# Output stage of a spectral layer: norms two tiles sooner, one norm on GpSimd, turns spread over tiles, one more tile's x added on TensorE

## The chip, the cores and the metric

One core of one Trainium2 chip runs the whole program. The metric is the device time of one execution in microseconds (us), lower is better. This document also measures *stage lengths* inside the profiles: from the first 128x256 matmul of an output stage to the first matmul of the MLP behind it. They repeat far better than the totals (the three kernels below that should have the same stage show 25.08 or 25.09 us six times), and the views of PE's waits name no transfer in that stretch. Each stage length comes from one profiled execution. "Fast" and "slow" are states of an execution: the one slow execution met here took 1254.71 us at a granted TensorE clock of 0.556, the fast ones of the same kernel 737.71 to 741.87 us at 0.992 to 0.995 (lib_switch).

Engines: TensorE (PE, with its weight loads PEld), VectorE (DVE), ScalarE (ACT), GpSimd (POOL), SyncE (SP).

## The reference, cut to what matters

```python
def reference(A_x, A_w_r, A_w_i, B_x, B_w1, B_b1, B_w2, B_b2):
    # _A_ref: rfft2 over (2048, 576), times a complex filter, irfft2
    # _B_ref: layernorm, x @ w1 + b1, gelu, @ w2 + b2     (576 -> 4608 -> 576)
    x = A_x
    x = x + _A_ref(_layernorm(x, axis=-1), A_w_r, A_w_i)
    x = x + _B_ref(_layernorm(x, axis=-1), B_w1, B_b1, B_w2, B_b2)
    x = x + _A_ref(_layernorm(x, axis=-1), A_w_r, A_w_i)
    x = x + _B_ref(_layernorm(x, axis=-1), B_w1, B_b1, B_w2, B_b2)
    return x
```

The Fourier transforms are matmuls with constant matrices. The **output stage** is the end of the inverse transform: for each of 16 tiles of 128 rows it makes the last two products, adds x, and, while that goes on, prepares the first four tiles (the "quad") for the MLP: layernorm, then a transposition ("turn") on PE. It runs twice, once per layer.

## The kernel before: the parts that matter

The program order is fixed by hand on every engine. PSUM is shared by a pool of three two-bank buffers (`big_ps`) and one of two small buffers (`sm_ps`). Cuts are marked.

```python
    class SpectralOut:
        early = (1, 2, 6, 10)          # tiles whose x is added by PE, not by VectorE

        def idft_v(self, n):           # first product of tile n: four 128x256 matmuls, cast by ACT
            pu = sm_ps([P, 2, 2, 128], F32) if fresh else self.st.pop(("pu", n))
            ...
            marks["u2", n] = nc.scalar.copy(out=u2[:], in_=pu[:]).ins

        def idft_v_rest(self, q):      # last 34 rows of four tiles: one buffer
            pr = sm_ps([P, 4, P], F32)
            ...                        # 64x128 matmuls
            nc.scalar.copy(out=u2r[:], in_=pr[:])

        def put_x(self, n):            # x of an early tile, four 128x288 matmuls
            po = big_ps([P, 2, 512])
            ...

        def idft_k(self, n):           # second product of tile n: six 128x288 matmuls
            ...

        def add(self, n):              # early: one ACT copy, two VectorE adds; else three adds
            ...

        def run_all(self, prep, loads):
            ...                        # sums for the moments: ACT, tiles 1 to 7
            pieces[10].append(prep.root)
            for i, m in enumerate((13, 14, 14)):
                pieces[m].append(lambda i=i: prep.turn(i, "act"))
            behind_add = {9: [prep.moments], 11: [prep.scale_sums, lambda: prep.norm(0, nc.vector)],
                          12: [lambda: prep.norm(2, nc.vector)]}
            pieces[12].append(lambda: prep.norm_act(1))
            pieces[13].append(lambda: prep.norm_act(3))
            ...
            for n in range(NT):
                if n == NT - 1:
                    prep.turn(3, "act")
                if n in self.early[2:]:
                    self.put_x(n)
                self.idft_k(n)
                self.add(n)
                for call in behind_add.get(n, ()):
                    call()
                if 0 < n < NT - 2:
                    self.idft_v(n + 2)
                if n % 4 == 1 and n + 3 < NT:
                    self.idft_v_rest(n // 4 + 1)
                for call in pieces[n]:
                    call()
            self.add(NT)

    class Prep:
        def norm_act(self, i):         # norm on ACT; the last 64 columns are copied on GpSimd
            ...
            nc.gpsimd.tensor_copy(out=xn[:, D:640], in_=xn[:, D - 64 : D])

        def norm(self, i, engine=nc.gpsimd):   # norm on VectorE, column copy on `engine`
            ...

        def turn(self, i, evac):       # five transpositions on PE, one copy out of PSUM
            pt = sm_ps([P, 5, P])
            for ci in range(5):
                nc.tensor.transpose(pt[:, ci, :], xn[:, ci * 128 : (ci + 1) * 128], ident[:])
            if evac == "act":
                nc.scalar.copy(out=self.yT[:, :, i * 128 : (i + 1) * 128], in_=pt[:])
```

A turn needs the *copied* last 64 columns of its tile for its fifth transposition. The MLP's first matmul needs all four turned tiles.

## Time and profile before

| | before |
|---|---|
| time, median of the 6 runs beside the changed kernel | 731.12 us (730.81 to 731.41) |
| span of the profiled run | 729.2 us |
| PE busy | 98% of the span |
| first output stage | 58.99 to 84.88: 25.89 us |
| second output stage | 414.52 to 440.41: 25.89 us |

The page of the kernel before, parts 1 and 4. Part 1 has each engine's busy time, its share of the span, and its number of instructions; part 4 says by engine what the chain of work that ended last was made of (a q behind an engine's name is its sequencer).

```profile
PE 718.1 (98%) x5078; PEld 456.9 (63%) x5078; DVE 267.0 (37%) x917; ACT 309.5 (42%) x534; POOL 79.5 (11%) x139
...
PE 95%; ACT 2%; DVE 1%; DMA 1%; issue 0%; SPq 0%; POOL 0%; ACTq 0%; POOLq 0%
```

PE bounds the kernel, so a change that takes no work off PE can only win what PE still waits for. Those places are seen in the timeline. Below is PE at the end of the first output stage, kernel before: start, length, engine, source line, operation, output and inputs, shape, count, and in brackets the idle time before it with what ended it. Line 895 is a turn, 753 the second product of a tile, 919 the MLP. (Lengths of PE overlap, so starts are what counts: the first row is 0.44 us long, and the next starts 0.28 us after it.)

```profile
82.06 0.44 PE L895 MATMUL pss_1479<-ident,xn 128*128 128x128 bf16 x5
82.34 0.44 PE L895 MATMUL pss_1486<-ident,xn 128*128 128x128 bf16 x5
83.66 0.44 PE L895 MATMUL pss_1493<-ident,xn 128*128 128x128 bf16 x5 [0.88 <-ACT yT_1408 L897]
...
84.88 0.38 PE L919 MATMUL psb_1514<-yT_1408,w_sb 128*128 128x512 bf16 x1
```

Two turns at once fill both small buffers; the third waits 0.88 us until ACT has copied one out. ACT is late because the last norm stands in front of its copies; this is ACT at that time:

```profile
82.14 0.88 ACT L862 ACTIVATE xn<-x_sb,shift,rs 128x576 bf16<-128x576 bf16 x1
82.91 0.69 ACT L897 COPY yT_1408<-pss_1479 128x640 bf16<-128x640 bf16 x1
83.48 0.72 ACT L897 COPY yT_1408<-pss_1486 128x640 bf16<-128x640 bf16 x1
84.13 0.69 ACT L897 COPY yT_1408<-pss_1493 128x640 bf16<-128x640 bf16 x1
```

### The profile page before, as it was taken

The numbers are of one execution on the slowest core, as the hardware profiler recorded it, in microseconds if no ns is written. First come the engines' busy times: TensorE is split into PE (matmuls) and PEld (weight loads), VectorE is DVE, ScalarE is ACT, GpSimd is POOL, SyncE is SP. The second block draws the span as 40 slices with busy tenths as digits, with TensorE's granted clock in tenths as the row PEclk, the third lists the DMA queues.
The fourth block names the chain that finished last, engine by engine and source line by source line (L and its number), as shares of the span: only waits on it lengthen the run. The fifth ranks groups of instructions, "written<-read, shape, count | busy, mean of one in ns | idle before, by whom it ended". The sixth has DMA issues, their size and how long they took to land.

```text
span 729.2 us, 12472 instructions
## 1 busy us (share of the span) xinstructions
PE 718.1 (98%) x5078; PEld 456.9 (63%) x5078; DVE 267.0 (37%) x917; ACT 309.5 (42%) x534; POOL 79.5 (11%) x139
## 2 busy tenths in 40 slices
PE   8999999999999999999999999999999999999998
PEld 5777645864587448744877674477447744774476
DVE  7894910664055504520367586011400140110011
ACT  7796764026411651156216686610550056005600
POOL 4240112002000200000006301200100010000000
PEclk9999999999999999999999999999999999999999
DMA  9788345211111111100217402530102010200000
GB/s 291 215 194 202 141 150 194 66 44 54 37 39 50 55 32 41 47 7 1 59 40 235 134 2 71 188 115 18 44 1 45 17 45 1 45 19 8 1 17 17
DMA packets 52722, 54.33 MB, mean 75 GB/s; under 512 B 31576, under 2 KB 43624, under 8 KB 52664
## 3 DMA queue, kind: packets, MB, share of 16 engines
q1 hardware_dynamic: 43784, 25.99, 13.5%
q0 software_dynamic: 8448, 26.96, 11.7%
q8 instruction: 40, 0.66, 0.4%
q10 hardware_dynamic: 432, 0.58, 0.2%
q14 instruction: 18, 0.15, 0.1%
HBM read 29.31 MB, written 8.59 MB: 52 GB/s over the span
## 4 chain that ended last, share of the span: by engine, by line
PE 95%; ACT 2%; DVE 1%; DMA 1%; issue 0%; SPq 0%; POOL 0%; ACTq 0%; POOLq 0%
PE psb_4486 L966 1%; PE psb_6902 L966 1%; PE psb_6304 L966 1%; PE psb_5706 L966 1%; PE psb_4228 L966 1%; PE psb_4100 L966 1%; PE psb_3294 L966 1%; PE psb_2492 L966 1%; PE psb_2126 L966 1%; PE psb_1998 L966 1%; PE psb_7654 L966 1%; PE psb_7577 L966 1%; PE psb_7500 L966 1%; PE psb_7185 L966 1%; PE psb_7108 L966 1%; PE psb_6587 L966 1%
## 5 line engine op out<-in xcount | busy, mean ns | idle before, releaser
L966 PEld LDWEIGHTS <-h_sb 128*128 128x128 bf16 x2304 | 224.9, 98 | 57.8 <-issue 0.2
L919 PEld LDWEIGHTS <-w_sb 128*128 128x128 bf16 x1152 | 109.5, 98 | 142.4 <-issue 17.2
L875 DVE TENSOR_SCALAR xn<-x_sb,mv,rs 128x576 bf16<-128x576 bf16 x24 | 9.4, 427 | 67.2 <-DMA quad_1818<-xn 28.9
L333 DVE BATCH_NORM_STATS2 stats<-x_sb 128x6 f32<-128x288 bf16 x78 | 30.8, 437 | 0.0
L927 PEld LDWEIGHTS <-w1r_sb 64*128 64x128 bf16 x288 | 10.8, 94 | 24.5 <-issue 17.0
L961 DVE TENSOR_TENSOR xb<-x_sb,b_bc 128x576 f32<-128x576 bf16 x32 | 24.0, 749 | 0.0
L878 POOL COPY xn<-xn 128x64 bf16<-128x64 bf16 x24 | 6.4, 268 | 150.7 <-DVE xn L875 150.7
L654 PEld LDWEIGHTS <-h_sb 128*128 128x128 bf16 x160 | 15.4, 97 | 5.5 <-DVE shared_721 L639 0.6
L933 ACT ACTIVATE h_sb<-psb_6064,b_sb 128x512 bf16<-128x512 f32 x2 | 1.3, 684 | 37.9 <-PE psb_6064 L927 37.9
L933 ACT ACTIVATE h_sb<-psb_7260,b_sb 128x512 bf16<-128x512 f32 x2 | 1.3, 684 | 37.8 <-PE psb_7260 L927 37.8
L933 ACT ACTIVATE h_sb<-psb_6662,b_sb 128x512 bf16<-128x512 f32 x2 | 1.3, 684 | 37.8 <-PE psb_6662 L927 37.8
L989 DVE TENSOR_TENSOR x_sb<-psb_7500,xb 128x576 bf16<-128x576 f32 x1 | 0.8, 758 | 43.4 <-PE psb_7500 L966 43.4
L989 DVE TENSOR_TENSOR x_sb<-psb_4100,xb 128x576 bf16<-128x576 f32 x1 | 0.8, 758 | 39.5 <-PE psb_4100 L966 39.5
L415 DVE TENSOR_TENSOR xf<-ef 128x256 bf16<-128x256 f32 (+1 forms) x56 | 13.6, 305 | 0.5
L621 PEld LDWEIGHTS <-c_f_84 128*128 128x128 bf16 x108 | 10.4, 97 | 4.4 <-DMA v_sb<-w_sb 1.1
L989 DVE TENSOR_TENSOR x_sb<-psb_6902,xb 128x576 bf16<-128x576 f32 x1 | 0.8, 757 | 33.6 <-PE psb_6902 L966 33.6
L989 DVE TENSOR_TENSOR x_sb<-psb_6304,xb 128x576 bf16<-128x576 f32 x1 | 0.8, 758 | 33.6 <-PE psb_6304 L966 33.6
L502 PEld LDWEIGHTS <-c_k_82 128*128 128x128 bf16 x112 | 10.4, 98 | 2.3
L989 DVE TENSOR_TENSOR x_sb<-psb_3294,xb 128x576 bf16<-128x576 f32 x1 | 0.8, 759 | 28.7 <-PE psb_3294 L966 28.7
L989 DVE TENSOR_TENSOR x_sb<-psb_2492,xb 128x576 bf16<-128x576 f32 x1 | 0.8, 758 | 28.7 <-PE psb_2492 L966 28.7
L833 ACT ACTIVATE h_sb<-x_sb 128x576 bf16<-128x576 bf16 x16 | 11.2, 700 | 0.1
L486 PEld LDWEIGHTS <-xT 128*128 128x128 bf16 x96 | 9.3, 97 | 3.1 <-issue 0.7
(1422 smaller groups left out, 1534.5 us busy)
## 6 DMA issues: line engine op xcount, KB each, us to landing
w_sb<-in_B_w_dram SPq DMA_DIRECT2D x16, 288.0 KB
v_sb<-in_B_w_dram POOLq DMA_DIRECT2D x4, 1152.0 KB, 6.5
shared_1512<-in_B_w_dram POOLq DMA_DIRECT2D x2, 1440.0 KB, 7.5
shared_5461<-in_B_w_dram POOLq DMA_DIRECT2D x2, 1440.0 KB, 7.6
out_dram<-x_sb SPq DMA_DIRECT2D x15, 144.0 KB
v_sb<-w_sb POOLq DMA_DIRECT2D x13, 145.0 KB, 4.9
x_sb<-in_A_x_dram SPq DMA_DIRECT2D x3, 576.0 KB
b_sb<-shared_721 POOLq DMA_DIRECT2D x11, 145.0 KB, 4.8
```

Of the source, the lines that this page charges most:

```text
L333: nc.vector.bn_stats(out=stats[:, h, :], in_=x_sb[:, t, h * DH : (h + 1) * DH])
L415: nc.vector.tensor_tensor(out=xf[:, at0 : at0 + 2 * n].rearrange("p (g d) -> p g d", g=2), in0=ef[:, :, first : first + n], in1=ef[:, :, b ...
L486: nc.tensor.matmul(pz[:, o, 0:KP], lhsT=xT[:, ci, :], rhs=c_fd[:, 3 * o + q, :], start=(q == 0), stop=(q == 2),)
L502: nc.tensor.matmul(py[:, r, 0:KP], lhsT=(c_k1_late if t in LATE else c_k1)[:, pl, :], rhs=z[:, ri], start=(q == 0), stop=(q == 1))
L621: nc.tensor.matmul(px[:, o, 0:KP], lhsT=c_f2[:, n // 4, pl, n % 4, :], rhs=vx[:, E_SLOTS.index(e), ri, :], start=(q == 0), stop=(q == 1))
L654: nc.tensor.matmul((ph, odd)[o][:, o, 0:KP], lhsT=i1[:, pl, n % 4, :], rhs=rhs, start=(q == 0), stop=(q == len(terms) - 1))
L833: nc.scalar.activation(out=at(h_sb, [P, D], 512 * 34), in_=x_sb[:, self.quad[i], :], func=(ACT.Copy, ACT.Square)[k], accum_out=self.s12[:, ...
L875: nc.vector.tensor_scalar(out=xn[:, 0:D], in0=x_sb[:, self.quad[i], :], scalar1=mean, scalar2=rs, op0=ALU.subtract, op1=ALU.mult)
L919: nc.tensor.matmul(acc[p][q], lhsT=w1_sb[:, ci, fc * 128 : (fc + 1) * 128], rhs=yT[:, ci, :], start=(first and ci == 0), stop=(not first a ...
L927: nc.tensor.matmul(acc[p][q], lhsT=w1r_sb[rows, p, :], rhs=yT[rows, 4, :], start=first, stop=not first)
L961: nc.vector.tensor_tensor(out=xb[:], in0=xr, in1=b2_bc[:].rearrange("p (h n) -> p h n", h=2), op=ALU.add)
L966: nc.tensor.matmul(parts[h][:, h, 0:DH], lhsT=hts[fc][:, i * 128 : (i + 1) * 128], rhs=w2_chunk(fc)[:, h * DH : (h + 1) * DH], start=(fc = ...
```

## The change

Intent: start the norm of the quad two tiles sooner so that the turns can stand at tiles 11, 12, 13 and 14, one each; give one norm to the idle GpSimd; take work off VectorE by letting PE add x of tile 13 as well; and free the start of the stage from a wait for a small PSUM buffer. The diff also moves two column copies: those of norms 0 and 2 stood on VectorE and now stand in GpSimd's queue, that of norm 2 behind the new norm.

```diff
-        early = (1, 2, 6, 10)
+        early = (1, 2, 6, 10, 13)
...
-            pr = sm_ps([P, 4, P], F32)
+            pr = (sm_ps if q else big_ps)([P, 4, P], F32)
...
-            pieces[10].append(prep.root)
-            for i, m in enumerate((13, 14, 14)):
-                pieces[m].append(lambda i=i: prep.turn(i, "act"))
-            behind_add = {9: [prep.moments], 11: [prep.scale_sums, lambda: prep.norm(0, nc.vector)], 12: [lambda: prep.norm(2, nc.vector)]}
-            pieces[12].append(lambda: prep.norm_act(1))
-            pieces[13].append(lambda: prep.norm_act(3))
+            behind_add = {8: [prep.moments], 9: [prep.scale_sums, lambda: prep.norm(0), lambda: prep.norm_pool(1)]}
+            pieces[8].append(prep.root)
+            pieces[10].append(lambda: prep.norm_act(2))
+            for n, i in ((11, 0), (12, 2), (13, 1), (14, 3)):
+                pieces[n].append(lambda i=i: prep.turn(i, "act"))
+            pieces[11].append(lambda: prep.norm_act(3))
...
-                if n == NT - 1:
-                    prep.turn(3, "act")
...
+        def norm_pool(self, i):
+            mean, rs = self.mr[i]
+            xn = work.tile([P, 640], BF16, tag="xn", bufs=3)
+            nc.gpsimd.tensor_scalar(
+                out=xn[:, 0:D], in0=x_sb[:, self.quad[i], :], scalar1=mean, scalar2=rs, op0=ALU.subtract, op1=ALU.mult
+            )
+            nc.gpsimd.tensor_copy(out=xn[:, D:640], in_=xn[:, D - 64 : D])
+            self.st[i] = xn
```

## The prediction

> **What bounds it now.** The page gives a span of 729.2 us with TensorE (PE) busy 98%; the chain of waits is 95% PE. The output stage runs twice: 57.4 to 84.9 us and 413 to 440.4 us. In the first, the timeline shows PE work back to back but for: 0.4 us before the four-tile buffer of the last rows (PE waits for ScalarE's (ACT) first cast), 0.2 us at tile 8, 0.3 us at tile 14, and 0.88 us before the quad's last turn, because three turns stand together at the end, share two small PSUM buffers, and their ACT copies (0.58 us apart) queue behind a norm (0.77 us). The last copy then holds the first MLP matmul 0.2 us. From tile 8's end on PE has about 10.0 us of work in 11.6 us.
>
> **What changes.** (1) Moments, root and scales come two tiles sooner, turns stand at tiles 11 to 14, one each: removes most of those 1.4 us. (2) x of tile 13 goes over PE: adds 0.5 us of PE per stage (four 128x288 matmuls, start to start as at tile 10), takes about 0.75 us off VectorE (DVE). (3) The first rows buffer no longer waits for a small PSUM buffer: saves about 0.2 us; the rest returns because tile 0's buffer must wait for the copy of the rows. (4) One norm goes to GpSimd. I replayed the tail by hand with the trace's durations: MLP would start about 1.0 us earlier, plus 0.2 us from (3): 1.2 us per stage, 2.3 us in all, if GpSimd is quick enough. That alone gives about 729.
>
> **The catch.** The changed program's order of instructions shows, on GpSimd in the first stage only, a library reload just before the tensor_scalar of the new norm. The kernel before has none.[...] It stands behind the column copy of norm 0 (about 77.8 us) and before norm 1 and the column copy of norm 2, which turn 2 (wanted at 79.9 us) needs. Estimate: [...]two copies at 0.24 us: turn 2 starts near 86.3, PE idles about 6.4 us. PE works in order, so all of it is critical. Such idle time also cools PE: at the kernel's start five 128x512 matmuls took 427 ns each, later 216 ns[...]. The remaining 4 us of the stage then run at half speed: about 2 us more. First stage: +7.3 us; second: -1.1 us. Net about +6.
>
> **Predicted:** 737.3 us, range 732 to 743. Faster by over 2%: 0.00; within 2%: 0.95; slower by over 2%: 0.05.
>
> **What would show it.** A PE wait of 5 to 9 us before turn 2 in the first stage, released by GpSimd, none in the second; GpSimd silent from about 78 to 85 us; matmuls of 240 ns instead of 122 ns just after. Second stage: first MLP matmul about 1.2 us sooner after the stage's start, the waits of 0.88 and 0.24 us gone.
>
> **What would make it wrong.** The reload may cost nothing because the library is already there (then 729), or twice as much (then 745). GpSimd's norm may take over 1.6 us, which would stall turn 2 in the second stage too. PE may stay warm (2 us less).

How long the reload and GpSimd's norm would take were the author's estimates, with no trace behind them, and the idle 6.4 us, the +7.3 us and the 737.3 us rest on them. That PE would run at half speed behind that idle time was an estimate too, from the matmuls at the kernel's start (427 against 216 ns); lib_switch2 below shows it (granted clock 0.52 behind a wait of 7.64 us).

## The result, and the profile after

Ratios here and below are the mean time of one kernel's fast runs over the mean of the other's fast runs of the same rounds, so not quite the ratio of the medians quoted.

| | before | after |
|---|---|---|
| time, median of 6 runs | 731.12 us | 730.39 us (729.48 to 731.63) |
| ratio, 95% interval | | 0.999 (0.9977 to 1.0003) |
| first stage | 25.89 us | 59.36 to 85.08: 25.72 us |
| second stage | 25.89 us | 415.46 to 441.01: 25.55 us |

The changed kernel is about as fast as the one before. The two stages are 0.17 and 0.34 us shorter. The predicted loss of 6 us did not happen, and neither did the gain of 2.3 us that was predicted for the case without that loss.

GpSimd at the end of the first stage, kernel after (885, 872 and 863 are column copies, 869 the new norm), and then in the second stage:

```profile
77.99 0.24 POOL L885 COPY xn<-xn 128x64 bf16<-128x64 bf16 x1 [22.95 <-DVE xn L882]
78.30 2.28 POOL L869 TENSOR_SCALAR xn<-x_sb,mean,rs 128x576 bf16<-128x576 bf16 x1
80.65 0.24 POOL L872 COPY xn<-xn 128x64 bf16<-128x64 bf16 x1
80.82 0.46 POOL L863 COPY xn<-xn 128x64 bf16<-128x64 bf16 x2
...
434.01 0.24 POOL L885 COPY xn<-xn 128x64 bf16<-128x64 bf16 x1 [24.08 <-DVE xn L882]
434.23 2.29 POOL L869 TENSOR_SCALAR xn<-x_sb,mean,rs 128x576 bf16<-128x576 bf16 x1
```

The reload of the library stands between the first two rows. The view of line 869 shows it on GpSimd's sequencer, as two instructions of 15 ns (length: least, median, most; then first and last start):

```profile
L869 POOLq MODIFY_POOL_CONFIG  x2: 15/15/15, 78.2 to 78.2; - x2
```

From the start of the column copy to the start of the norm it is 0.31 us with the reload and 0.22 us in the second stage without it. So here the reload costs 0.09 us. The norm, on the other hand, takes 2.28 us, over the 1.6 us that the prediction had named as the limit (VectorE makes norm 0 in 0.42 us, at 77.43 us of the same profile), and it stands in front of the column copy of norm 2. PE at that time, kernel after (902 is a turn, 741 is x of tile 13, 926 the MLP):

```profile
79.73 0.60 PE L696 MATMUL pss_1445<-c_r_85,b_sb 128*128 128x256 bf16 x4
80.27 0.38 PE L902 MATMUL pss_1452<-ident,xn 128*128 128x128 bf16 x4
81.11 0.23 PE L902 MATMUL pss_1452<-ident,xn 128*128 128x128 bf16 x1 [0.45 <-POOL xn L863]
81.18 0.65 PE L741 MATMUL psb_1459<-x_sb,halves 128*128 128x288 bf16 x4
...
83.85 0.44 PE L902 MATMUL pss_1497<-ident,xn 128*128 128x128 bf16 x5
...
85.08 1.89 PE L926 MATMUL psb_1518<-yT_1352,w_sb 128*128 128x512 bf16 x7
```

Four transpositions of turn 2 run; the fifth, on the copied columns, waits for GpSimd. From the four 128x256 matmuls in front of turn 2 to x of tile 13 it is 1.45 us here (79.73 to 81.18) and 1.28 us in the second stage (435.83 to 437.11). In copy2_dve below, where nothing waits for GpSimd, it is 0.81 and 0.82 us, so the wait costs 0.64 and 0.46 us. (The texts below say 0.7 and 0.55. They count the turn from the end of those matmuls; about 0.1 us of that is a wait for a small PSUM buffer, which ACT frees at 80.22 us, and it stays in copy2_dve.) The old 0.88 us wait before the last turn is gone in both.

Why the profiled span rose (729.2 to 729.8 us) while the stages shrank: the first stage began 0.37 us later (59.36 against 58.99), and PE waited longer at the head of the second stage. That wait (in total, times, longest, in us), before and then after:

```profile
PE pss_5026 L696 <- DMA v_sb<-h_sb: 0.7, 1, 0.7
```

```profile
PE pss_5030 L696 <- DMA v_sb<-h_sb: 1.4, 1, 1.4
```

This wait for a transfer lies before the stage begins. It was 0.2 to 1.4 us in the profiles, with no pattern by edit. It is probably part of why totals scatter by 1 to 2 us; that share was not measured. The stage lengths leave it out, and so they decide below.

### The profile page after: what moved, and what is told of

Read it like the earlier page. It is cut to its first block, busy times and chain, and to the rows that moved or that the text cites. A ratio compares the mean times of both kernels' runs of the same rounds, so it can differ in the third digit from the quotient of the medians.

```text
span 729.8 us, 12461 instructions
## 1 busy us (share of the span) xinstructions
PE 717.5 (98%) x5052; PEld 457.6 (63%) x5086; DVE 264.8 (36%) x909; ACT 310.1 (42%) x536; POOL 84.8 (12%) x145
## 4 chain that ended last, share of the span: by engine, by line
PE 89%; DMA 3%; DVE 3%; ACT 2%; issue 1%; POOL 1%; SPq 1%; ACTq 0%; DVEq 0%; POOLq 0%
PE psb_4490 L973 1%; PE psb_5714 L973 1%; PE psb_3298 L973 1%; PE psb_2932 L973 1%; PE psb_2496 L973 1%; PE psb_2130 L973 1%; PE psb_7662 L973 1%; PE psb_7585 L973 1%; PE psb_7508 L973 1%; PE psb_7193 L973 1%; PE psb_7116 L973 1%; PE psb_7038 L973 1%; PE psb_6910 L973 1%; PE psb_6595 L973 1%; PE psb_6518 L973 1%
```

## The experiments

All start from the changed kernel unless said otherwise; all gave correct results. Stage lengths are first / second. Each batch ran with the kernel before beside it, whose medians were 731.23, 731.22 and 731.49 us.

| run | time, us | ratio to before (95%) | stages, us |
|---|---|---|---|
| kernel before | 731.12 | 1 | 25.89 / 25.89 |
| kernel after | 730.39 | 0.999 (0.9977 to 1.0003) | 25.72 / 25.55 |
| copy2_dve | 729.23 | 0.9974 (0.9962 to 0.9986) | 25.08 / 25.09 |
| pool_order | 729.25 | 0.9976 (0.9962 to 0.9989) | 25.08 / 25.08 |
| norm1_dve | 729.40 | 0.9969 (0.9957 to 0.9982) | 25.08 / 25.09 |
| turn3_mid | 729.15 | 0.9968 (0.9955 to 0.9982) | 25.12 / 25.12 |
| split3 | 730.09 | 0.9986 (0.9974 to 0.9999) | 25.27 / 25.25 |
| no_x13 | 730.79 | 0.9992 (0.998 to 1.0004) | 25.82 / 25.57 |
| copy2_no_x13 | 731.16 | 1.0004 (0.9991 to 1.0016) | 25.58 / 25.49 |
| rows_small | 731.03 | 0.9997 (0.9985 to 1.001) | 25.77 / 25.61 |
| before_x13 (from before) | 731.55 | 1.0002 (0.999 to 1.0015) | 26.58 / 26.30 |
| pool_probe, one look | 731.26 | | 25.63 / 25.53 |
| lib_switch, 3 fast runs | 737.71, 739.31, 741.87 | 1.0117 (1.0096 to 1.0138) | |
| lib_switch2, one look | 739.39 | | 35.03 / 25.54 |

### Is it the place behind GpSimd's norm? copy2_dve

```diff
-            pieces[10].append(lambda: prep.norm_act(2))
+            pieces[10].append(lambda: prep.norm_act(2, nc.vector))   # column copy of norm 2 on VectorE; cut: norm_act passes the engine on
```

> Edit: the changed kernel, but the column copy of norm 2 runs on VectorE, so turn 2 no longer stands behind GpSimd's norm 1 (2.28 us in the profile of after). Theory A (the gain was lost to that wait, 0.7 us in the first stage and 0.55 in the second): the stage from its first 128x256 matmul to the first MLP matmul falls from 25.72 and 25.55 us to about 24.9 and 25.0, no PE wait for GpSimd is left, time about 729.1 (ratio to before about 0.997). Rival B (PE's extra matmuls for tile 13 and VectorE's adds set the end of the stage, the wait only hides it): stage lengths unchanged within 0.2 us, a new wait appears before a later turn or before the MLP, time about 730.4.

Measured: 25.08 and 25.09 us, 729.23 us. The view of PE's waits has no row between the stage's first matmul and the MLP. The copy on VectorE took 0.17 us, and PE went through turn 2 without a stop:

```profile
78.81 0.17 DVE L863 COPY xn<-xn 128x64 bf16<-128x64 bf16 x1
```

```profile
79.32 0.60 PE L696 MATMUL pss<-c_r,b_sb 128*128 128x256 bf16 x4
79.86 0.44 PE L902 MATMUL pss<-ident,xn 128*128 128x128 bf16 x5
80.13 0.65 PE L741 MATMUL psb<-x_sb,halves 128*128 128x288 bf16 x4
```

Theory A holds: 0.64 and 0.46 us per stage come back with one small copy moved. The stage lengths came out 0.1 to 0.2 us longer than expected.

### Is it GpSimd's slowness or only the order of its queue? pool_order, norm1_dve

```diff
-            behind_add = {8: [prep.moments], 9: [prep.scale_sums, lambda: prep.norm(0), lambda: prep.norm_pool(1)]}
+            behind_add = {8: [prep.moments], 9: [prep.scale_sums, lambda: prep.norm(0)]}
-            pieces[10].append(lambda: prep.norm_act(2))
+            pieces[10] += [lambda: prep.norm_act(2), lambda: prep.norm_pool(1)]
```

> Edit: the changed kernel with norm 1 still on GpSimd, but recorded after norm 2, so that GpSimd makes norm 2's column copy first. If it is the place in the queue and not the engine that cost the time: turn 2 does not wait, norm 1 ends about 81.8 us, just as turn 1 wants it, stages 25.1 to 25.3 us, time 729.2 to 729.6. If GpSimd's norm is too slow in any place: turn 1 waits over 0.4 us instead, stages 25.5 us or more, time about 730.4.

Measured: 25.08 us twice, 729.25 us. GpSimd in pool_order:

```profile
78.84 0.24 POOL L863 COPY xn<-xn 128x64 bf16<-128x64 bf16 x1 [0.98 <-PE pss L902]
79.15 2.29 POOL L869 TENSOR_SCALAR xn<-x_sb,mean,rs 128x576 bf16<-128x576 bf16 x1
81.50 0.24 POOL L872 COPY xn<-xn 128x64 bf16<-128x64 bf16 x1
```

The norm is as slow as before, but turn 1 starts at 81.84 us, just after its column copy. So the engine was not too slow for this norm; the queue had the wrong order.

For norm1_dve the edit is `prep.norm_pool(1)` to `prep.norm(1)`: the norm on VectorE, no arithmetic left on GpSimd.

> Edit: the changed kernel with norm 1 on VectorE (0.42 us) in place of GpSimd (2.28 us); the column copies stay on GpSimd. If GpSimd's norm in front of norm 2's column copy is the whole loss: no wait for GpSimd, stages 25.1 us as in copy2_dve and pool_order, time about 729.3. If VectorE has no room for it (the reason to use GpSimd at all): stages 25.4 us or more with a wait for VectorE.

Measured: 25.08 and 25.09 us, 729.40 us, no wait for VectorE. VectorE had room for the 0.42 us. Giving this norm to GpSimd brought nothing; it only made the mistake in the order possible.

### Does GpSimd need 2.28 us by itself? pool_probe

```diff
             keep_busy(7, big_ps)
+            nc.gpsimd.tensor_scalar(            # scratch output, nobody reads it
+                out=at(h_sb, [P, D], NFC * 512 - D), in0=x_sb[:, order[-1], :], scalar1=c_eps[:, 0:1], scalar2=c_eps[:, 1:2],
+                op0=ALU.subtract, op1=ALU.mult,
+            )
             self.idft_v(0)
```

> Edit: the changed kernel with one more tensor_scalar of the norm's size (128x576 bf16, scratch output) on GpSimd at the head of each output stage, while VectorE has nothing to do for some 6 us. Theory A (GpSimd itself needs 2.28 us for it): 2.28 us here too. Rival B (VectorE's operations[...] slow it): 1.0 to 1.5 us here, 2.28 us in the tail. The reload moves to the head of the first stage; norm 1 then starts 0.22 us after the column copy in both stages, and the time stays near 730.4.

The 1.0 to 1.5 us of rival B were the author's estimate, not shown by any run. GpSimd in the first stage (line 800 is the probe, 889 and 873 the column copy and the norm), where VectorE had only two casts out of PSUM to do, from 55.22 to 55.78 us, and nothing more until 62.65:

```profile
54.89 2.30 POOL L800 TENSOR_SCALAR h_sb<-x_sb,c_eps 128x576 bf16<-128x576 bf16 x1
77.76 0.24 POOL L889 COPY xn<-xn 128x64 bf16<-128x64 bf16 x1 [20.57 <-DVE xn L886]
77.98 2.28 POOL L873 TENSOR_SCALAR xn<-x_sb,mean,rs 128x576 bf16<-128x576 bf16 x1
```

2.30 us beside a nearly idle VectorE (2.29 in the second stage) and 2.28 us beside a busy one: the norm costs that by itself, rival B falls. The norm now starts 0.22 us after the copy in the first stage as well, as expected with the reload at the probe.

### What would a real reload have cost? lib_switch, lib_switch2

```diff
             keep_busy(7, big_ps)
+            if not switched:                    # once, in the first stage
+                switched.append(1)
+                sw = work.tile([P, 2], F32, tag="sw", bufs=1, name="sw")
+                nc.gpsimd.partition_broadcast(sw[:], c_eps[0:1, :])
             self.idft_v(0)
```

(The line that sets `switched = []` is cut.) The program then has two reloads: of another library before the broadcast, and of the former one before the norm.

> Edit: the changed kernel with one small GpSimd operation of another library (a broadcast over partitions into a scratch tile) at the head of the first output stage, where GpSimd is idle for 20 us. The reload before norm 1 now has to bring a library back; in the profile of after it took 15 ns twice and norm 1 began 0.31 us after the start of the column copy before it (0.22 us in the second stage, which has no reload). Theory A (the predicted reload costs nothing because the library was still there; a real one costs what the recorded prediction said): norm 1 begins 6 to 8 us after the column copy, PE waits 5 to 7 us before turn 2, the matmuls after that run at half speed (128x288 every 240 ns instead of 122), time 737 to 740. Rival B (a reload is cheap here in any case): gap under 0.5 us, time about 730.4.

The 6 to 8 us of theory A were the author's estimate, with no trace behind them; lib_switch2 gives 6.98. The three fast runs took 737.71 to 741.87 us. A fourth, the profiled one, was in a slow state: 1254.71 us, granted clock 0.76 in its first 10 us and 0.55 to 0.56 in every later stretch asked for, so from far ahead of the edit. Nothing is concluded from its time. (GpSimd's norm took 2.30 us in it, against 2.28 to 2.29 in the fast kernel after.)

> The same kernel as lib_switch, again, because the one run that was profiled there fell into a slow state of 1254.7 us at a granted clock of 0.556 from the first microseconds on; its GpSimd[...] needed 7.03 us from the column copy to norm 1. Expected in a fast run: norm 1 again 7 us after the column copy, PE waits 5 to 6 us before turn 2 in the first stage only, matmuls after it slower for 2 to 4 us, time 737 to 742 as the three fast runs gave. If PE stays at full speed behind the wait, the time is about 736.

Measured: 739.39 us, a single run of unknown state, at a mean granted clock of 0.995 and inside the range of the three fast runs. GpSimd, then PE, in the first stage:

```profile
60.54 0.26 POOL L804 PARTITION_BROADCAST sw<-c_eps  x1 [5.89 <-issue]
77.45 0.24 POOL L890 COPY xn<-xn 128x64 bf16<-128x64 bf16 x1 [16.65 <-DVE xn L887]
84.66 2.30 POOL L874 TENSOR_SCALAR xn<-x_sb,mean,rs 128x576 bf16<-128x576 bf16 x1 [6.98 <-issue]
```

```profile
87.74 0.29 PE L907 MATMUL pss<-ident,xn 128*128 128x128 bf16 x1 [7.64 <-POOL xn L868]
87.82 1.17 PE L742 MATMUL psb<-x_sb,halves 128*128 128x288 bf16 x4
88.78 0.69 PE L754 MATMUL psb<-c_gd,u 128*128 128x288 bf16 x2
...
92.20 0.41 PE L754 MATMUL psb<-c_gd,u 128*128 128x288 bf16 x2
...
93.79 2.53 PE L931 MATMUL psb<-yT,w_sb 128*128 128x512 bf16 x10
```

Here is everything that had been predicted for the changed kernel, in a kernel where the library really had to come back: 6.98 us in which GpSimd stands still (and 5.89 us before the broadcast), a PE wait of 7.64 us before the last part of turn 2 (5 to 7 had been expected), and slow matmuls behind it until about 92 us. PE works in order: x of tile 13, which needs nothing of turn 2, started only behind it, at 87.82 us (80.13 in copy2_dve). It took 0.96 us start to start (87.82 to 88.78) instead of 0.49. From the last transposition of turn 2 to the MLP it was 6.05 us (87.74 to 93.79) against 3.97 in the kernel after (81.11 to 85.08), so the slow stretch cost 2.1 us.

The reload itself is no longer in the profile than the free one, 11 ns twice, so its length says nothing of its cost. Only the gap behind it does:

```profile
L874 POOLq MODIFY_POOL_CONFIG  x2: 11/11/11, 77.7 to 77.7; - x2
```

The view by stretches of the same profile shows the clock (length, then the busy times of PE, PEld, DVE, ACT and POOL, then the granted clock, DMA share and GB/s):

```profile
75.00:80.00 5.00, 5.00 (x57) 4.05 (x51) 4.85 (x14) 4.41 (x9) 0.24 (x1) 1.00 0.75 277
80.00:85.00 5.00, 0.10 (x2) 0.00 (x0) 1.59 (x5) 0.90 (x2) 0.34 (x1) 1.00 0.01 2
85.00:90.00 5.00, 2.26 (x11) 1.46 (x12) 0.00 (x0) 0.69 (x1) 4.16 (x5) 0.52 0.01 2
90.00:95.00 5.00, 4.90 (x33) 3.41 (x33) 2.80 (x6) 3.52 (x5) 0.00 (x0) 0.79 0.00 0
```

By estimate from these rows, with 0.50 for the slow clock, as the halved pace of the 128x288 matmuls suggests (0.24 against 0.12 us), the clock fell at 85.2 us, about 5 us after PE had gone idle, and was back at 92.1 us. A reading of 1.00 does not always mean full pace: in the first 2 us of the kernel before the view says 1.00, though 512-column matmuls started every 0.43 us there against 0.22 us later.

The stage grew from 25.72 to 35.03 us, 9.3 us; the second stage stayed at 25.54 us. So theory A holds and rival B falls: the reload is dear when another library is there (6.98 us), and nearly free when the wanted one is (0.09 us in the kernel after).

### What is x of tile 13 on PE worth? no_x13, copy2_no_x13, before_x13

The edit in the first two is `early = (1, 2, 6, 10)` again; the second has copy2_dve's edit too.

> Edit: the changed kernel without x of tile 13 on TensorE (VectorE adds it as before). A: the GpSimd wait stays (0.7 and 0.55 us); PE has 0.49 us less after it, but the first MLP matmul then waits for tile 13's adds on VectorE; by hand 0.2 us shorter stages, time about 730.0. B (the extra matmuls ate the gain): stages 0.5 us shorter each, time about 729.4, with no wait for VectorE.

> Both edits together. A: PE is ready for the MLP about 0.5 us sooner than with the first edit alone, but waits for VectorE's add of tile 13: stages about 25.1 us, time 729.1 to 729.6, so x of tile 13 on TensorE is worth nothing or a little. B: the savings add up, stages 24.4 us or less, time about 728.3.

Measured: 25.82 / 25.57 us, and 25.58 / 25.49 us. In no_x13 PE's last product starts 0.50 us sooner after the stage's first matmul than in the kernel after (24.89 against 25.39 us). In copy2_no_x13 it is only 0.11 us sooner than in copy2_dve (24.64 against 24.75): PE stops twice just until an ACT copy ends and frees a small PSUM buffer (copies to 81.34 and 81.93 us, PE on at 81.39 and 81.99). In both, PE then waits for VectorE at the MLP's first matmul, whose PSUM buffer was that of tile 13 and was still being added. The MLP's start in the timeline of PE, copy2_no_x13; the wait is in the bracket:

```profile
84.83 2.53 PE L926 MATMUL psb<-yT,w_sb 128*128 128x512 bf16 x11 [0.65 <-DVE x_sb L782]
```

With the wait for GpSimd removed, x of tile 13 on PE is worth 0.5 and 0.4 us per stage (25.58 against 25.08, 25.49 against 25.09). Expected had been "nothing or a little"; that expectation was wrong, because VectorE's chain to tile 13's last add ended later than my hand sum had it. With the GpSimd wait in place (no_x13) it is worth 0.1 us or less, where it had been expected to cost 0.2 us.

The same part alone on the kernel before:

> Edit: the kernel before with x of tile 13 on TensorE, and nothing else. In the kernel before the end of the stage is set by ACT (norms and three copies in a row), so 0.49 us more on PE is partly hidden in the waits there: stages 25.9 to 26.2 us against 25.89, time 731.2 to 731.8. If VectorE's lag set the end of the stage in the kernel before: stages shorter than 25.7 us, time below 730.8.

Measured: 26.58 and 26.30 us, 0.7 and 0.4 us longer than the kernel before, even a little over what was expected. There the end is set by ACT's row of norms and copies, and the stall before the last turn (0.91 us) stays. An early tile also gives ACT a copy, which neither the prediction nor this expectation had counted. It takes 0.39 us and stands in just that row (80.91 us in this run), between norm 1 and the copies out of PSUM; ACT's last copy ends 0.70 us later after the stage's first matmul than in the kernel before. How much of this is ACT's copy and how much PE's extra matmuls was not tested apart. The part pays only together with the earlier norms.

### The rows buffer: rows_small

The edit is `pr = sm_ps([P, 4, P], F32)` again.

> Edit: the changed kernel with the first rows buffer back in the small PSUM pool. The recorded prediction gave the big buffer 0.2 us per stage (then 730.8 here). The profile of after says 0.06: from the stage's first matmul to the end of tile 0's product 3.26 us against 3.32 before. Theory now: 3.32 again, time about 730.5, not to be told from 730.4.

Measured: 25.77 / 25.61 us against 25.72 / 25.55: the big buffer is worth about 0.05 us per stage. The wait for ACT's first cast (0.24 us) is back, but with the big buffer tile 0 waits for the copy of the rows instead, for nearly as long. The times cannot tell them apart.

### Two attempts at the last 0.2 us: split3, turn3_mid

In copy2_dve and pool_order the MLP starts 0.2 us after PE could. split3 (from copy2_dve) splits the last turn's copy out of PSUM between ACT and VectorE (the lines that move this turn ahead of tile 14's adds are cut):

```diff
+            if evac == "split":
+                cols = slice(i * 128, (i + 1) * 128)
+                nc.vector.tensor_copy(out=self.yT[:, 3:5, cols], in_=pt[:, 3:5])
+                nc.scalar.copy(out=self.yT[:, 0:3, cols], in_=pt[:, 0:3])
```

> Edit: norm 2's column copy on VectorE (run copy2_dve: stages 25.08 and 25.09 us), and the last turn's copy out of PSUM split between ACT (three blocks) and VectorE (two), recorded ahead of tile 14's adds. In copy2_dve PE ended about 83.8 us and the MLP began 84.03, when ACT's copy was done. Expected: the MLP begins right behind PE's last product, stages 24.9 us, time about 0.4 us less than copy2_dve. If VectorE's adds are the next limit instead: stages unchanged or longer, with a wait for VectorE before the MLP.

Measured: 25.27 / 25.25 us, longer. ACT's part waited for VectorE's part, though they write different blocks:

```profile
83.39 0.29 DVE L907 COPY yT<-pss 128x256 bf16<-128x256 bf16 x1 [0.55 <-PE pss L904]
```

```profile
83.71 0.48 ACT L908 COPY yT<-pss 128x384 bf16<-128x384 bf16 x1 [0.45 <-DVE yT L907]
```

The two parts are disjoint blocks of one tile, and yet the program had a wait between them; why is not shown. The run says nothing about the idea itself.

turn3_mid (from pool_order) puts the last turn between the two halves of tile 14's product (cut: the argument in `idft_k`, and the removal of this turn from its old place):

```diff
-                self.idft_k(n)
+                self.idft_k(n, (lambda: prep.turn(3, "act")) if n == NT - 2 else None)
```

> Edit: as pool_order (norm 1 behind norm 2 on GpSimd, stages 25.08 us), and the last turn between the two halves of tile 14's product on TensorE, so that ACT's last copy ends before TensorE's last product. In pool_order the MLP starts about 0.2 us after that product. Expected: stages 24.9 us, time 0.3 us less than pool_order's 729.25, which five rounds hardly resolve; the stage lengths decide. If the turn waits for the small PSUM buffer that ACT frees about then: stages 25.1 us or more.

Measured: 25.12 us twice. The MLP now follows PE's last product at once, but PE stood still for a quarter of a microsecond before the turn (the matmul before it started at 82.90, the turn at 83.27), until ACT had freed the small buffer at 83.2 us. The wait moved, nothing was won; the alternative is what happened.

## Why the prediction was wrong, point by point

- **The step that failed** is the time set down for the reload on the critical path, an estimate of the author's that no trace had shown. In the changed kernel the reload took 0.09 us, and the PE wait before turn 2 was 0.45 us and not 6.4. The first stage became 0.17 us shorter and not 7.3 us longer. The listed alternative, "the reload may cost nothing because the library is already there (then 729)", was the true one, and the prediction gave it too little weight. That the library was there is inferred: the same instruction costs 6.98 us once another library has been used (lib_switch2) and 0.09 us otherwise.
- **What followed from that step** was right as a chain of causes and had nothing to act on. lib_switch2 shows each link: predicted idle PE 6.4 us, measured 7.64; predicted 4 us at half speed that cost 2 us, measured some 4 us that cost 2.1; predicted stage 1 +7.3 us against before, measured +9.1 (35.03 against 25.89), partly because the norm takes 2.3 us, more than had been counted.
- **GpSimd's norm was mis-sized.** Its size was the author's estimate, with no trace named for it; measured 2.28 us in the first stage, 2.29 in the second, and 2.30 beside a nearly idle VectorE. The prediction named 1.6 us as the limit above which turn 2 would stall in the second stage too. It did, by 0.46 us; the first stage lost 0.64 us. copy2_dve, pool_order and norm1_dve each undo this, by three different edits, and land on the same 25.08 us.
- **The gain without the catch was oversized.** Predicted 1.2 us per stage; with the stall removed it is 0.81 (25.89 to 25.08). The rows buffer brings 0.05 and not 0.2; the rest of the difference is at the tail, where 1.0 had been counted and about 0.75 came.
- **x of tile 13:** its cost of 0.5 us on PE was right, and so was the idea that it pays by relieving VectorE; the copy of 0.4 us that it puts on ACT had been left out. Without it the stage is 0.4 to 0.5 us longer, although PE has 0.49 us less to do, because the MLP then waits 0.65 us for VectorE. This shows only where GpSimd's queue is in order.
- **"Within 2%"** was right, as any value near 730 would have been.

So the answer to "where did the gain go": of 0.81 us per stage, 0.64 and 0.46 us were given back as a new wait behind GpSimd's norm, for a column copy that the change itself had moved into that queue. The best versions (copy2_dve, pool_order, norm1_dve, turn3_mid; not to be told apart) are about 2 us faster than the kernel before by their times. Against the changed kernel the intervals of the times still touch; the stage lengths say 1.1 us (0.64 and 0.46).

## What to carry to other kernels

An engine that seems free still has a queue: before giving it a long operation, look for short ones behind it that another engine is waiting for, and put those first. Size the operation by a trace of the same operation on the same engine, and where there is none, treat the size as the main risk. A reload in the program's text is not a load on the chip: it took 0.09 us where the library was there, and where it was not it took 6.98 us, with some 4 us of TensorE at half pace behind the wait, so ask which library was used last before counting it.
